# A fused mLSTM cell and tanh-shrink MLP on one core: the steady part begins at the first half-done group instead of the second

## The chip, the cores and the metric

The kernel runs on one core of one Trainium2 chip. The metric is device time in microseconds (us) of one execution, the median of several; lower is better. PE is the engine that multiplies matrices, PEld its weight loads, DVE the vector engine, ACT the scalar engine with the activation functions, POOL the general engine, SP the engine whose queue here only issues transfers. Each engine works through its own list of instructions in the order in which they stand. Matrix products land in banks of PSUM, and ACT or DVE must have read a bank before PE may fill it again.

## The reference

Two stages follow each other. The first is an mLSTM cell over 4 batches, 8 heads, 768 time steps and head size 40; the second is an MLP over the 3072 rows of 320 numbers that the cell gives.

```python
for t in range(S):                                   # per batch and head
    m_new  = max(f[t] + m, i[t])
    f_stab = exp(f[t] + m - m_new);  i_stab = exp(i[t] - m_new);  m = m_new
    C = f_stab * C + i_stab * outer(v[t], k[t])
    n = f_stab * n + i_stab * k[t]
    y[t] = sigmoid(o_gate[t]) * (C @ q[t]) / max(|n . q[t]|, 1)
x = y.transpose(0, 2, 1, 3).reshape(B * S, H * D)    # 3072 x 320
h = x @ w_in                                         # 320 x 2048
out = (h - tanh(h)) @ w_out                          # 2048 x 320
```

The weights come as 64-bit floats; the kernel turns them into 32-bit floats on the chip.

## The kernel before

**Units, groups, pairs, items.** The cell is cut into 24 units, each 128 time steps of one batch with all heads; unit n is time block n // 4 of batch n % 4. Two units make a group of 256 rows of x, so there are 12 groups, 0 to 11. The 2048 columns of `w_in` are cut into 8 pairs of 128-column blocks, 0 to 7. One group times one pair is a run, and PE works on items of two runs (the first two items have one): the products with `w_in` (called up, into the PSUM banks `ph_up`, one for each block of a pair), then h - tanh(h) as a polynomial on ACT and DVE, then the products with `w_out` (called down, into `po` or `pS`). There are 49 items. On the rows of x of a small group, `RUNS` walks along diagonals: items 0 to 8 hold pairs 0 to 3 of groups 0 to 3, items 9 and 10 pairs 4 to 7 of group 0, items 11 and 12 those of group 1, 13 and 14 of group 2, 15 and 16 of group 3; from item 17 on each group has four items.

**The polynomial.** For an item ACT computes z (`square`) and q (`again`) from `ph_up`; DVE computes `gt<-ph_up,z` twice (here called the cubes; the first cube is the last reader of the first `ph_up` bank, so the next item's first product waits for it), then `gt<-q,gt` twice. Pairs 4 to 7, and all pairs from group 4 on, use a scheme of seven products in place of eight for down: DVE first forms four sums of gt (`s1` to `s4`, in `sums_of_g`) and, once for each pair of `w_out`, four differences of blocks of it (`wT`, in `sums_of_weights`). `put_together` makes the output `ob` of a group from the banks `pS` and, for groups 0 to 3, from the parts of pairs 0 to 3 (`part`).

**Planned part and steady part.** The first part of the program is laid out by a planner (`Plan`): it holds operations with estimated times, ranks, tokens for buffers, and it records them in the order in which its own model starts them. It covers the weights' conversion from 64 bits, the units below `PLANNED`, and the items below `START`. Where it finds PE idle, it puts in products that compute nothing (`awake`). From item `START` on a loop walks item by item in a fixed order, and DVE's and ACT's other work (the list `work`) is merged in at places that are given in items. `START` is the item that holds run (`TAIL`, `SPLIT`), so `TAIL`, 2 and `SPLIT` 4 make it item 13.

**What differs in the steady part.** There x is split into two parts, x and l, with their difference d (`split_x`), the weights of a pair into high, low and cross parts (`split_in`: four steps, ACT, DVE, ACT, DVE), and up is 24 products in a faster number format (names `x_thirds`, `thirds`, `w_thirds`, `w_high`) plus eight halves in place of eight full products plus halves (`in_thirds`). The products of x and of l come first, those of d last; between them ACT rescales each bank (`ph_up<-ph_up`). An item falls back to full products if its pairs are not split by then. Pairs 4 and 5 are split in the planned part, 6 half there, 7 and 0 to 3 in the steady part. A pair's low and cross part are eight blocks of 128 x 128 that need homes in memory that something else has left (`homes`).

A unit, too, is computed in another way in the steady part: `crossed_scores` (tile `ps`) in one item and `block_turned` (tiles `pT`, `pc`) in the next, with `turn_back` and `gate_turned` on DVE and two trips through memory (`h_rows`, `z_in` and `y_rows`, `xT`) in place of the products that the planned part spends on turning. `cell_slot` sets, in 21 places over two items, where the parts of the unit before (its gates) come.

**Order on the queues.** Within each engine the order is pinned as recorded. SP issues the loads of the planned units and the units' trips through memory; POOL issues the loads of weights, of the units in the steady part, and the stores of `ob`.

Of the kernel before, what the change touches and what calls it, by code (L numbers as in the profile page):

```python
# [49 lines left out]
FP = mybir.dt.float32  # L50
# [11 lines left out]
L = 128  # L62
# [26 lines left out]
def kernel(  # L89
# [215 lines left out]
    FIRST, SPLIT, PLANNED, TAIL = 4, 4, 10, 2  # L305
# [65 lines left out]
    padded = {}  # L371

    def load_unit(n, names=("kz", "qz", "v", "k", "o", "q2"), queue=SP, behind=(), crossed=False):
# [3 lines left out]
        for name in names:  # L377
# [3 lines left out]
            elif name in ("kz", "qz"):  # L381
                t[name] = load.tile([128, HH, L], FP, name=name, tag=f"{name}{n % 3 if n < PLANNED and not general else n % 2}", bufs=1)
# [298 lines left out]
    def scaled(n, i, name, bufs, by_heads=False):  # L681

        t = un[n]
        flat = padded["vs"][n % 4] if t["crossed"] else att.tile([L, H * D1 + HALF - D1], FP, name=name, tag="P" if general else name, bufs=bufs)
# [217 lines left out]
    def turn_back(n):  # L902
# [3 lines left out]
        both = att.tile([128, 2, HH * L // BLOCK, BLOCK], FP, name="zt", tag="P", bufs=4)  # L906
# [12 lines left out]
        t["z"] = att.tile([L, 2, H, BLOCK], FP, name="z_in", tag="P", bufs=4)  # L919
# [31 lines left out]
    def cell_slot(s, o):  # L951
# [12 lines left out]
        steps += 6 * pause  # L964
# [4 lines left out]
        return steps + 4 * pause  # L969
# [168 lines left out]
    def homes(p):  # L1138

        def at(tag, pool=const, n=4):  # L1140
            if tag not in places:
                places[tag] = pool.tile([128, n, 128], FR, name="w_thirds", tag=tag, **({} if pool is const else {"bufs": 1}))

        if p == 4:
            at("space", n=9)
        elif p == 5:
            at("kz2", load)
            at("qz2", load)
        elif p == 6:
            at("part0", n=5)  # L1150
            at("q2", n=9)
        elif p == 7:
            at("diag")
            for b in range(2):
                at(f"state{(PLANNED + b) % B}", n=2)
        elif p == 0:
            for b in range(2, B):
                at(f"state{(PLANNED + b) % B}", n=2)
            at("part1", n=5)
        elif p == 1:  # L1160
            at("xT2", n=6)
        elif p == 2:
            at("xT3", n=6)
            at("part2", n=5)
        else:
            at("part3", n=5)
        four = range(4)
        blocks = [(tag, n) for tag, ns in (
            (*((f"state{(PLANNED + b) % B}", range(2)) for b in (2, 3)), ("part1", four)),
            (("xT2", range(6)), ("part0", (4,)), ("part1", (4,))),  # L1170
            (("xT3", four), ("part2", four)),
            (("part3", four), ("xT3", (4, 5)), ("part2", (4,)), ("part3", (4,))),
            (("space", range(8)),),
            (("kz2", four), ("qz2", four)),
            (("part0", four), ("q2", (6, 7, 8)), ("space", (8,))),
            (("diag", four), *((f"state{(PLANNED + b) % B}", range(2)) for b in (0, 1))))[p] for n in ns]
        return blocks[0:4], blocks[4:8]
# [523 lines left out]
    def plan_thirds():  # L1701
# [328 lines left out]
```

## Time and profile before

| | us |
|---|---|
| median of 3 runs | 499.57 (498.94 to 509.22) |
| profiled execution, its own time | 495.56 |
| span of the profiled execution, first to last instruction | 493.8 |
| around the span | 1.8 |
| first product of item 13, the first of the steady part | 165.4 from the span's start |
| first product of item 20 | 231.4 |
| first product of item 48, the last | 474.7 |

A span begins at 0. A row of the timeline has the start, the time, the engine, the program's names of what is written and read, and how many instructions were merged; in brackets the idle time before it and what ended that. Products overlap, so what a stretch of PE takes is read from the start of its first row to the start of the row behind it, not from the sum of the times; the same holds for DVE, whose instructions overlap by some 0.08 us. A number behind an x in a timeline counts instructions as the chip ran them, where a full 32-bit product is two; the lists of order count it once.

Where PE's units stand in the span: its busy share by 40 equal slices is 9 tenths or more in each but the last, and DVE's is lower.

```
PE   9999999999999999999999999999999999999995
DVE  5999969998977697999897886996995988775734
ACT  4566597676455435455454544444545445454541
POOL 4523304320003341523423423431241100000000
```

### The profile page before, as it was taken

To read this page: it belongs to the slowest core of one execution; us is meant where nothing else is said; L and a number is where in the kernel's file an instruction comes from. 1 tells how busy PE (TensorE), PEld (TensorE's weight loads), DVE (VectorE), ACT (ScalarE), POOL (GpSimd) and SP (SyncE) were. 2 spreads that over 40 slices of the span, in tenths; PEclk is the share of its full clock that TensorE was granted. 3 is DMA by queue.
4 is the path that set the end of the run, shared out by engine and by line. 5 is a ranking of instruction groups with operands and counts; after the bars stand their busy time and mean duration, and the time that the engine had idled before them with its cause. 6 is when DMAs were issued, how large, how long until landed. Compare 5 with 4: busy or idle time off the path is not lost.

```text
span 493.8 us, 12474 instructions
## 1 busy us (share of the span) xinstructions
PE 483.7 (98%) x4715; PEld 431.1 (87%) x4715; DVE 400.8 (81%) x913; ACT 256.2 (52%) x609; POOL 119.3 (24%) x221
## 2 busy tenths in 40 slices
PE   9999999999999999999999999999999999999995
PEld 5778888787788898898999999999999999999995
DVE  5999969998977697999897886996995988775734
ACT  4566597676435455545454444544545445454541
POOL 4523304320003341523423423431241100000000
PEclk9999999999999999999999999999999999999998
DMA  7987625740001223355346436444444432420001
GB/s 232 286 261 246 191 71 142 149 136 7 7 1 35 61 65 74 101 118 125 81 98 140 99 83 137 99 98 103 95 112 83 94 82 44 75 60 1 27 1 33
DMA packets 116902, 48.82 MB, mean 99 GB/s; under 512 B 96872, under 2 KB 109064, under 8 KB 116836
## 3 DMA queue, kind: packets, MB, share of 16 engines
q1 hardware_dynamic: 107132, 23.21, 23.1%
q0 software_dynamic: 9504, 24.43, 16.4%
q8 instruction: 39, 0.64, 0.5%
q10 hardware_dynamic: 200, 0.33, 0.2%
q14 instruction: 27, 0.22, 0.1%
HBM read 37.30 MB, written 10.35 MB: 97 GB/s over the span
## 4 chain that ended last, share of the span: by engine, by line
PE 88%; DVE 6%; ACT 2%; DMA 1%; issue 1%; SPq 0%; DVEq 0%; ACTq 0%
PE ph_up L138 36%; PE pS L138 29%; PE po L138 7%; PE ph L138 4%; PE ps L138 3%; PE awake L138 3%; PE pT L138 3%; PE pc L138 2%; DVE gt L115 1%; DVE s L115 1%; PE px L142 1%; DVE w_thirds L115 1%; DMA h_rows<-zt 1%; DVE zt L115 1%; ACT q L115 0%
## 5 line engine op out<-in xcount | busy, mean ns | idle before, releaser
L115 ACT ACTIVATE z<-ph_up 128x512 f32<-128x512 f32 (+1 forms) x98 | 56.8, 583 | 102.5 <-PE ph_up L138 97.0
L115 ACT ACTIVATE ph_up<-ph_up 128x512 f32<-128x512 f32 x70 | 40.7, 582 | 82.4 <-PE ph_up L138 79.1
L115 DVE SCALAR_TENSOR_TENSOR gt<-ph_up,z 128x512 f32<-128x512 f32 (+1 forms) x98 | 62.7, 671 | 22.9 <-ACT z L115 22.7
L138 PE MATMUL pS<-wT,s 128*128 128x160 f32 x480 | 71.9, 299 | 0.0
L138 PEld LDWEIGHTS pS<-wT,s 128*128 128x128 f32 x480 | 67.4, 190 | 0.3 <-issue 0.2
L115 ACT ACTIVATE q<-z,tiny 128x512 f32<-128x512 f32 (+1 forms) x98 | 65.8, 711 | 0.7
L115 DVE SCALAR_TENSOR_TENSOR gt<-q,gt 128x512 f32<-128x512 f32 (+1 forms) x98 | 63.5, 677 | 0.0
L115 POOL DMA_DIRECT2D out<-ob x11 | 8.0, 727 | 220.6 <-DVE ob L115 220.6
L138 PE MATMUL pS<-w_out,gt 128*128 128x160 f32 x320 | 58.4, 312 | 0.0
L138 PE MATMUL ph_up<-xT,w_half 64*64 64x256 f32 (+1 forms) x608 | 53.6, 393 | 0.0
L138 PEld LDWEIGHTS pS<-w_out,gt 128*128 128x128 f32 x320 | 45.4, 189 | 5.4 <-issue 3.6
L138 PE MATMUL ph_up<-x_thirds,w_high 128*128 128x256 f32 x280 | 47.9, 293 | 2.0 <-DVE gt L115 2.0
L138 PE MATMUL ph_up<-xT,w_in 128*128 128x256 f32 x208 | 49.0, 382 | 0.0
L138 PE MATMUL ph_up<-x_thirds,w_thirds 128*128 128x256 f32 x280 | 44.4, 281 | 0.0
L138 PEld LDWEIGHTS ph_up<-xT,w_in 128*128 128x128 f32 x208 | 38.5, 190 | 5.4
L138 PEld LDWEIGHTS ph_up<-x_thirds,w_high 128*128 128x128 f32 x280 | 38.5, 188 | 2.7 <-PE pS L138 2.1
L138 PE MATMUL ph_up<-thirds,w_thirds 128*128 128x256 f32 x250 | 39.8, 292 | 0.2 <-ACT ph_up L115 0.2
L138 PEld LDWEIGHTS ph_up<-xT,w_half 64*64 64x64 f32 (+1 forms) x608 | 28.1, 146 | 12.9 <-issue 3.7
L138 PE MATMUL po<-w_out,gt 128*128 128x320 f32 x128 | 38.2, 441 | 0.0
L138 PEld LDWEIGHTS ph_up<-x_thirds,w_thirds 128*128 128x128 f32 x280 | 37.9, 188 | 0.0
L138 PEld LDWEIGHTS ph_up<-thirds,w_thirds 128*128 128x128 f32 x250 | 33.3, 189 | 0.4 <-ACT ph_up L115 0.4
L138 PEld LDWEIGHTS po<-w_out,gt 128*128 128x128 f32 x128 | 23.1, 190 | 8.7 <-issue 0.7
(143 smaller groups left out, 870.0 us busy)
## 6 DMA issues: line engine op xcount, KB each, us to landing
w<-in_moe_w_out POOLq DMA_DIRECT2D x8, 640.0 KB, 6.4
w<-in_moe_w_in POOLq DMA_DIRECT2D x16, 256.0 KB, 4.7
h_rows<-zt SPq DMA_DIRECT2D x56, 64.0 KB
z_in<-h_rows SPq DMA_DIRECT2D x56, 64.0 KB
out<-ob POOLq DMA_DIRECT2D x11, 320.0 KB, 2.7
y_rows<-yt SPq DMA_DIRECT2D x56, 48.0 KB
xT<-y_rows SPq DMA_DIRECT2D x28, 96.0 KB
kz<-in_kT POOLq DMA_DIRECT2D x26, 80.0 KB, 2.8
```

Source lines behind the costliest of these rows:

```text
L115: i = method(*args, **kwargs)
L138: return cls.keep(nc.tensor.matmul(*args, **kwargs))
L142: return cls.keep(nc.tensor.transpose(*args, **kwargs))
```

## The change

The steady part now begins at item 11 (`TAIL` 1) and takes over unit 9 (`PLANNED` 9). The rest follows from this or goes with it:

- x's parts get another home: x in `P3`, one of four buffers of the units, which are now named one by one and taken in turn (`next_p`), four in the planned part and three in the steady part; l in `xT0`. `xT1` holds group 1, which is still in use.
- The parts of pairs 5, 6, 7 and 0 to 3 get other homes, and are begun at other places, in items from `START`: pairs 0 to 3 at 1.6, 2.6, 4.4 and 5.4 (2.0, 3.0, 5.4 and 6.6 before). Most pairs' parts lie in fewer pieces, so one instruction takes the place of two or three. `s1` and `s3` share a buffer, since pair 5 takes the one of `s3`.
- The differences of `w_out` for pairs 0 to 3 (16 instructions on DVE) leave the planned part, and stand in the steady part at 2.2, 3.7, 5.5 and 6.3 items from `START`.
- In `cell_slot` the gates come two places of 21 later, with two pauses fewer behind them.

```diff
-    FIRST, SPLIT, PLANNED, TAIL = 4, 4, 10, 2
+    FIRST, SPLIT, PLANNED, TAIL = 4, 4, 9, 1
...
-    padded = {}
+    padded, turns_of_p = {}, [0, 4]
+
+    def next_p():
+        turns_of_p[0] += 1
+        return f"P{turns_of_p[0] % turns_of_p[1]}"
...
-        un[n]["P"] = att.tile([L, 2, HH, L], FP, name="P", tag="P", bufs=4)
+        un[n]["P"] = att.tile([L, 2, HH, L], FP, name="P", tag=next_p(), bufs=1)
...
-        steps += 6 * pause
+        steps += 8 * pause
...
-        return steps + 4 * pause
+        return steps + 2 * pause
...
-        s1, s2, s3 = (conv.tile([128, 2, L], FP, name=name, tag=tag, bufs=2)[:, 0:len(some)]
-                      for name, tag in (("s1", "w_e"), ("s2", "w_m"), ("s3", "w_r")))
+        two = conv.tile([128, 2, 2, L], FP, name="s1", tag="w_e", bufs=2)
+        s1, s3 = two[:, 0, 0:len(some)], two[:, 1, 0:len(some)]
+        s2 = conv.tile([128, 2, L], FP, name="s2", tag="w_m", bufs=2)[:, 0:len(some)]
...
         elif p == 5:
-            at("kz2", load)
-            at("qz2", load)
+            for name in ("one", "two"):
+                at(name, 5, conv, "w_r", 2)
...
-        x, l = (const.tile([128, NK + 1, TG], FR, name="x_thirds", tag=f"xT{k}") for k in range(2))
+        x = att.tile([128, NK + 1, TG], FR, name="x_thirds", tag="P3", bufs=1)
+        l = const.tile([128, NK + 1, TG], FR, name="x_thirds", tag="xT0")
...
-                              ([op] if op else [converted[p, 0], *seconds, *([results[0]] if p == 6 else [])]) + ([uses] if i == 2 else []), 60.0 if i < 2 else -12.0)
+                              ([op] if op else [*converted.values(), *seconds]) + ([uses] if i == 2 else []), 60.0 if i < 2 else -12.0)
...
-        op = None
-        for p in range(SPLIT):
-            steps_of_p = []
-            for i in range(2):
-                op = plan.add("V", 0.65, lambda p=p, i=i, steps=steps_of_p: [steps.extend([] if i else sums_of_weights(p)), *[step() for _, step in steps[2 * i:2 * i + 2]]],
-                              [op] if op else [made[NP - 1]], 70.0)
...
+    turns_of_p[1] = 3
...
-    for p, x0 in ((6, -0.25), (7, 0.1), (0, 2.0), (1, 3.0), (2, 5.4), (3, 6.6)):
+    for p, x0 in ((6, -0.25), (7, 0.1), (0, 1.6), (1, 2.6), (2, 4.4), (3, 5.4)):
...
+    for p, x0 in ((0, 2.2), (1, 3.7), (2, 5.5), (3, 6.3)):
+        sums_of_p = []
+        for i in range(4):
+            work[START + int(x0 + 0.15 * i)].append((START + x0 + 0.15 * i, 0.0, lambda p=p, i=i, steps=sums_of_p: [steps.extend(() if i else sums_of_weights(p)), steps[i][1]()]))
```

What this moves is shown at three places. The first is PE's list at the end of the planned part. Before, item 12's up is followed by the beginning of item 11's down (`pS_1681`, `pS_1683`), and then by twenty `awake` products, each with its own weight load; this is where they begin:

```order
L138 MATMUL pS_1552<-w_out,s_1601 128x160 x2
L138 MATMUL ph_up<-xT,w_in 128x256 x8
L138 MATMUL ph_up<-xT,w_half 128x256 x4
L138 MATMUL pS_1681<-w_out,gt 128x160 x4
L138 MATMUL pS_1683<-wT,gt 128x160 x2
L138 LDWEIGHTS diag
L138 MATMUL awake<-diag 128x512
```

The same engine now, behind item 8's down: the second of two `awake`, item 10's up, item 9's down (`pS_1478` to `pS_1480`), and with the third row from the end the steady part begins, at item 11:

```order
L138 LDWEIGHTS diag
L138 MATMUL awake<-diag 128x512
L138 MATMUL ph_up<-xT,w_in 128x256 x8
L138 MATMUL ph_up<-xT,w_half 128x256 x4
L138 MATMUL pS_1478<-w_out,gt 128x160 x4
L138 MATMUL pS_1480<-wT,gt 128x160 x2
L138 MATMUL pS_1479<-wT,s_1463 128x160 x4
L138 MATMUL pS_1478<-wT,s_1464 128x160 x2
L138 MATMUL pS_1480<-w_out,s_1465 128x160 x2
L138 MATMUL ph_up<-x_thirds,w_high 128x256 x4
L138 MATMUL ph_up<-x_thirds,w_thirds 128x256 x4
L138 MATMUL ph_up<-x_thirds,w_high 128x256 x4
```

So no filler stands between the last planned down and the steady part. Over the whole list `awake` goes from 63 to 42 products; items 11, 12 and 18 change from full products to split ones; and unit 9's products change from the planned to the steady kind.

The second place is ACT's list where the steady part begins. Before, the upper part of x of the first steady group (`x_thirds<-xT`) stands behind item 10's polynomial, two items ahead of its use:

```order
L115 ACTIVATE z,sums<-ph_up 128x512
L115 ACTIVATE q<-z,tiny 128x512
L115 ACTIVATE z,sums<-ph_up 128x512
L115 ACTIVATE q<-z,tiny 128x512
L115 ACTIVATE x_thirds<-xT 128x768
L115 COPY w_high<-w_thirds 128x512 x2
```

Now it stands behind item 10's polynomial again, but item 10 is the last planned item, and the copies to `w_high` of pairs 4 and 5 stand ahead of it:

```order
L115 COPY w_high<-w_thirds 128x512
L115 ACTIVATE z,sums<-ph_up 128x512
L115 COPY w_high<-w_thirds 128x512
L115 ACTIVATE q<-z,tiny 128x512
L115 ACTIVATE z,sums<-ph_up 128x512
L115 ACTIVATE q<-z,tiny 128x512
L115 ACTIVATE x_thirds<-xT 128x768
L115 COPY vs<-crossed 128x8
```

So the first steady item needs what ACT does last in the planned part.

The third place is DVE's list from the sums of item 16 to the cubes of item 17. Before:

```order
L115 TENSOR_TENSOR s_2375<-s_2374,gt 128x256
L115 TENSOR_TENSOR s_2377<-gt,s_2375 128x256
L115 TENSOR_TENSOR P<-ps,over 128x384 x2
L115 TENSOR_TENSOR vs<-v,crossed 128x8x40
L115 SCALAR_TENSOR_TENSOR gt<-ph_up,z 128x512 x2
```

Now the differences of `w_out` of pairs 2 and 3 and the last step of pair 3's parts stand in between:

```order
L115 TENSOR_TENSOR s_2437<-gt,s_2436 128x256
L115 TENSOR_TENSOR wT<-w_out,wT 128x160
L115 SCALAR_TENSOR_TENSOR w_thirds<-w_thirds 128x512
L115 TENSOR_TENSOR wT<-w_out 128x160
L115 TENSOR_TENSOR wT<-w_out,wT 128x160
L115 TENSOR_TENSOR P<-ps,over 128x384 x2
L115 TENSOR_TENSOR vs<-v,crossed 128x8x40
L115 TENSOR_TENSOR wT<-w_out 128x160
L115 SCALAR_TENSOR_TENSOR gt<-ph_up,z 128x512
L115 TENSOR_TENSOR wT<-w_out,wT 128x160
L115 SCALAR_TENSOR_TENSOR gt<-ph_up,z 128x512
```

So the first cube comes five instructions later behind the sums, and another one stands between the two cubes.

More of the change, by code (lines that the diff above doesn't have):

```diff
@@ L381, in load_unit @@
             elif name in ("kz", "qz"):
-                t[name] = load.tile([128, HH, L], FP, name=name, tag=f"{name}{n % 3 if n < PLANNED and not general else n % 2}", bufs=1)
+                t[name] = load.tile([128, HH, L], FP, name=name, tag=f"{name}{(n + 1) % 3 if n < PLANNED and not general else n % 2}", bufs=1)
                 for i in range(2):
@@ L905, in turn_back @@
         t = un[n]
-        both = att.tile([128, 2, HH * L // BLOCK, BLOCK], FP, name="zt", tag="P", bufs=4)
+        both = att.tile([128, 2, HH * L // BLOCK, BLOCK], FP, name="zt", tag=next_p(), bufs=1)
         zt, added = both[:, 0], both[:, 1].rearrange("p b i -> p (b i)")
@@ L1138, in homes, with at @@
     def homes(p):
-        def at(tag, pool=const, n=4):
-            if tag not in places:
-                places[tag] = pool.tile([128, n, 128], FR, name="w_thirds", tag=tag, **({} if pool is const else {"bufs": 1}))
+        def at(name, n=4, pool=const, tag=None, bufs=1):
+            if name not in places:
+                places[name] = pool.tile([128, n, 128], FR, name="w_thirds", tag=tag or name, **({} if pool is const else {"bufs": bufs}))
+        first, second, third, fourth = (f"state{(PLANNED + i) % B}" for i in range(B))
@@ L1144, in homes @@
         if p == 4:
-            at("space", n=9)
+            at("space", 9)
         elif p == 5:
-            at("kz2", load)
-            at("qz2", load)
+            for name in ("one", "two"):
+                at(name, 5, conv, "w_r", 2)
         elif p == 6:
-            at("part0", n=5)
-            at("q2", n=9)
+            at("kz2", 4, load)
+            at("qz2", 4, load)
         elif p == 7:
             at("diag")
-            for b in range(2):
-                at(f"state{(PLANNED + b) % B}", n=2)
+            at(first, 2)
@@ L1156, in homes @@
+            at(second, 2)
         elif p == 0:
-            for b in range(2, B):
-                at(f"state{(PLANNED + b) % B}", n=2)
-            at("part1", n=5)
+            at("part0", 5)
         elif p == 1:
-            at("xT2", n=6)
+            at(third, 2)
+            at(fourth, 2)
+            at("xT1", 6)
         elif p == 2:
-            at("xT3", n=6)
-            at("part2", n=5)
-        else:
[L1166 to L1172, printed above, removed]
+            at("xT2", 6)
+        else:
+            at("part1", 5)
+            at("part2", 5)
@@ L1173, in homes @@
+        two, four = range(2), range(4)
+        blocks = [(name, n) for name, ns in (
+            (("part0", four), ("q2", (6, 7, 8)), ("part0", (4,))),
+            ((third, two), (fourth, two), ("xT1", four)),
+            (("xT2", range(6)), ("xT1", (4, 5))),
+            (("part1", four), ("part2", four)),
             (("space", range(8)),),
+            (("one", four), ("two", four)),
             (("kz2", four), ("qz2", four)),
-            (("part0", four), ("q2", (6, 7, 8)), ("space", (8,))),
@@ L1176, in homes @@
-            (("diag", four), *((f"state{(PLANNED + b) % B}", range(2)) for b in (0, 1))))[p] for n in ns]
+            (("diag", four), (first, two), (second, two)))[p] for n in ns]
         return blocks[0:4], blocks[4:8]
@@ L1893, in keep_any @@
         decay = eT[:, n].unsqueeze(2).to_broadcast([TOP, H, D1])
-        own = att.tile([TOP, H, D1], FP, name="own", tag="P", bufs=4)
+        own = att.tile([TOP, H, D1], FP, name="own", tag=next_p(), bufs=1)
         V.memset(own, 1.0)
```

10 lines of the change are left out of this document (5 added, 5 removed).

## The prediction

> **What bounds the kernel now.** I read the page's busy times first, then PE's waits, the sums by stage, and then the timelines of PE and DVE around the start of the steady part.
>
> ```profile
> PE 483.7 (98%) x4715; PEld 431.1 (87%) x4715; DVE 400.8 (81%) x913; ACT 256.2 (52%) x609; POOL 119.3 (24%) x221
> PE ph_up L138 <- DVE gt L115: 2.0, 3, 0.9
> 95.50:165.40 69.90, 69.90 (x398) 55.68 (x395) 60.77 (x133) 38.33 (x90) 12.12 (x31) 1.00 0.17 48
> 165.40:231.40 66.00, 63.57 (x782) 58.60 (x782) 57.47 (x134) 34.89 (x87) 21.67 (x39) 1.00 0.38 91
> 231.40:303.80 72.40, 72.38 (x929) 68.57 (x929) 60.49 (x145) 35.21 (x83) 26.00 (x46) 1.00 0.48 106
> ```
>
> PE bounds the kernel: 483.7 of 493.8 us. The next line is the largest of its waits, three times for DVE's gt. The last three are stages: length, then busy time (and count) of PE, PEld, DVE, ACT and POOL, the granted clock, the DMA share and GB/s. The end of the planned part (95.5 to 165.4) has PE without a gap, but some of that is `awake`, which computes nothing. Items 13 to 19 (165.4 to 231.4) have all the waits, with DVE busy for 57.5 of 66.0 us; from item 20 on PE is never without work. So a gain has to come from PE's own time or from those waits, and DVE is the engine that can give it back.
>
> **The planned part.**
>
> ```profile
> 95.56 1.06 PE L138 MATMUL ps<-qz,kz 40*128 40x128 f32 x16
> ...
> 121.03 0.55 PE L142 MATMUL px<-ident,ys 128*128 128x128 f32 x3
> ...
> 134.75 1.03 PE L138 MATMUL awake<-diag 128*128 128x512 bf16 x4
> 135.61 3.62 PE L138 MATMUL ph_up<-xT,w_in 128*128 128x256 f32 x16
> ...
> 141.96 1.79 PE L138 MATMUL pS<-wT,s 128*128 128x160 f32 x12
> ...
> 144.13 3.62 PE L138 MATMUL ph_up<-xT,w_in 128*128 128x256 f32 x16
> ...
> 158.99 4.48 PE L138 MATMUL awake<-diag 128*128 128x512 bf16 x20
> 163.31 1.79 PE L138 MATMUL pS<-wT,s 128*128 128x160 f32 x12
> 164.94 0.71 PE L138 MATMUL pS<-w_out,s 128*128 128x160 f32 x4
> 165.38 0.74 PE L138 MATMUL ph_up<-x_thirds,w_high 128*128 128x256 f32 x4
> ```
>
> Up to 95.56 PE's list is the same. Unit 9's planned products go: nine rows between 95.56 (`ps`, 0.98 to the next start) and 121.03 (`px`, 0.39), together 4.36 from start to start. Items 11 and 12 with items 10's and 11's down go (144.13 to 158.99 and 163.31 to 165.38): 14.86 + 2.07 = 16.93. Of 24 `awake` in this stretch three stay; 20 take 4.32 (158.99 to 163.31), so 0.216 each, and 21 give 4.53. The sum is 25.8, and item 11 could begin at 165.38 - 25.82 = 139.56, if PE alone decides.
>
> Unit 9's rows and one `awake`, 4.36 + 0.22, stand ahead of item 9's sums, so PE would want these at 141.96 - 4.6 = 137.4.
>
> ```profile
> 136.44 0.42 DVE L115 TENSOR_TENSOR s<-gt,s 128x256 f32<-128x256 f32 x1
> ```
>
> DVE had the last of them at 136.86, five us to spare. Ahead of them it loses unit 9's state, gates and scaling, two differences of `w_out` and one part of a pair's weights, 3.5 us by their rows, so it has them at 133.4 if its own list decides, with four to spare. The end that costs nothing is 0. The other end is that the conversions of the weights come no sooner than before, since they wait for transfers: then the sums end at 136.9 again, three steps on parts of pairs, item 10's polynomial and l follow, 5.6 together, and l comes at 142.5 in place of 140.1, some 2.4 us lost. I take 0: PE waits for DVE nowhere between 95.5 and 158.99.
>
> At item 11 there is a wait. PE's last planned up ends at 135.65; behind it ACT does z, a copy, q, z, q and then the upper part of x.
>
> ```profile
> 148.84 0.60 ACT L115 ACTIVATE z<-ph_up 128x512 f32<-128x512 f32 x1 [0.44 <-PE ph_up L138]
> ...
> 150.19 0.58 ACT L115 ACTIVATE z<-ph_up 128x512 f32<-128x512 f32 x1
> ```
>
> The first z and q with what stands between take 150.19 - 148.84 = 1.35 from start to start. With 0.6 for the copy and 0.8 for x (by DVE's 768 columns of it, below) the upper part ends at 135.75 + 2 x 1.35 + 0.6 + 0.8 = 139.85, and l follows on DVE at 140.9. PE wants x at 139.56 and l at 140.1, so it waits about 0.7 in all. Before, x was ready two items ahead. The ends of this wait are 0 and the 2.4 above.
>
> **The items that come back, and item 18.**
>
> ```profile
> 174.37 0.73 PE L138 MATMUL ph_up<-x_thirds,w_high 128*128 128x256 f32 x4
> ...
> 177.18 0.51 PE L138 MATMUL ph_up<-thirds 128*128 128x256 f32 x2 [0.20 <-ACT ph_up L115]
> ...
> 178.77 0.62 PE L138 MATMUL pT<-qz,state 40*64 40x128 f32 x16
> ...
> 191.92 0.71 PE L138 MATMUL pS<-w_out,s 128*128 128x160 f32 x4
> 193.38 0.71 PE L138 MATMUL ph_up<-x_thirds,w_high 128*128 128x256 f32 x4 [0.76 <-DVE gt L115]
> ...
> 201.91 0.71 PE L138 MATMUL pS<-w_out,s 128*128 128x160 f32 x4
> 202.98 0.74 PE L138 MATMUL ph_up<-x_thirds,w_high 128*128 128x256 f32 x4 [0.36 <-DVE gt L115]
> ...
> 212.71 3.62 PE L138 MATMUL ph_up<-xT,w_in 128*128 128x256 f32 x16
> ...
> 217.17 0.62 PE L138 MATMUL pT<-qz,state 40*64 40x128 f32 x16
> ...
> 229.79 0.71 PE L138 MATMUL pS<-w_out,s 128*128 128x160 f32 x4
> 231.42 0.71 PE L138 MATMUL ph_up<-x_thirds,w_high 128*128 128x256 f32 x4 [0.93 <-DVE gt L115]
> ```
>
> An undisturbed steady item with half a unit in it takes 174.37 - 165.38 = 8.99; items 11 and 12 with unit 9 so cost 17.98, against 21.29 in the planned kind. Item 13 then begins at 139.56 + 0.7 + 17.98 = 158.24, that is 7.1 sooner. Item 18 changes from full to split products: its up takes 217.17 - 212.71 = 4.46 now, item 14's 178.77 - 174.37 = 4.40 with a wait of 0.20 in it, so 0.3 is gained. The other work of items 13 to 48 is the same on PE.
>
> The waits of before: `pS<-w_out,s` takes 0.44 to the next start where nothing waits (164.94 to 165.38), and 1.46, 1.07 and 1.63 ahead of items 16, 17 and 20. That is 1.02 + 0.63 + 1.19 = 2.84 that could go.
>
> **DVE in the steady part.** This is where I expect part of it back.
>
> ```profile
> 127.94 0.32 DVE L115 TENSOR_TENSOR wT<-w_out 128x160 f32<-128x160 f32 x1
> 128.30 0.33 DVE L115 TENSOR_TENSOR wT<-w_out,wT 128x160 f32<-128x160 f32 x1
> 128.54 0.32 DVE L115 TENSOR_TENSOR wT<-w_out 128x160 f32<-128x160 f32 x1
> ...
> 189.23 1.02 DVE L115 TENSOR_TENSOR P<-ps,over 128x384 f32<-128x384 f32 x2 [1.04 <-PE ps L138]
> ...
> 191.87 0.76 DVE L115 SCALAR_TENSOR_TENSOR w_thirds<-w_thirds 128x256 fp32r<-128x256 f32 x2 [1.23 <-ACT w_high L115]
> 192.55 1.28 DVE L115 SCALAR_TENSOR_TENSOR gt<-ph_up,z 128x512 f32<-128x512 f32 x2
> 193.75 1.28 DVE L115 SCALAR_TENSOR_TENSOR gt<-q,gt 128x512 f32<-128x512 f32 x2
> 194.95 0.75 DVE L115 TENSOR_TENSOR s<-gt 128x256 f32<-128x256 f32 x2
> ...
> 215.67 0.48 DVE L115 TENSOR_TENSOR ob<-pS,a 128x320 f32<-128x320 f32 x1
> ...
> 217.47 0.83 DVE L115 TENSOR_TENSOR ob<-ob,part 128x640 f32<-128x640 f32 x1
> L115 DVE TENSOR_TENSOR thirds<-x_thirds 128x768 fp32r<-128x768 f32 x2 | 1.9, 948 | 0.0
> ```
>
> From start to start a cube is 0.60, a `gt<-q,gt` 0.60, a difference 0.24 to 0.36, a step of half a pair's parts 0.34 to 0.40. An item's polynomial and sums come to 4.0 to 4.4, the output of one of groups 0 to 3 to 2.4, the split of a group's x to 1.7, a pair's parts to 1.4, and a unit to 5 over two items. With these I summed DVE's order from each item's cubes to the next one's: after the change 8.0, 11.1, 9.0, 10.8, 9.0, 12.1 and 7.8 us for items 11 to 17, together 67.7, and then 8.2, 5.9, 9.0, 6.7. PE needs 9.0 an item, so 63 for these seven. (Before, items 13 to 19 have 8.0, 9.3, 9.5, 9.3, 8.0, 9.6, 7.1, so 60.8.) Three groups' outputs and x in pairs of items, six pairs' parts and the 16 differences now fall together.
>
> An excess costs PE only when the first cube comes after PE has done the item's down. At item 12 that leaves 1.5 us, and item 11 adds 1.0. Item 12's excess (11.1 - 9.0) uses this up; item 13 is level, but its step on pair 1's parts waits some 1.2 for ACT, whose first step on them stands behind item 13's q, and so item 14 waits 0.9. Item 14's excess then goes straight to item 16: 1.75. Item 16's (3.1) makes item 17's d of x 0.6 late and item 18's first product 2.45. From then on DVE needs less than PE. The sum is 5.7. The ends: 0, as from item 20 on before; and 12.5, if DVE's waits of before (1.23 for ACT, 1.04 for `ps`, above) come back at each of four pairs' parts and three units, 8.0 in place of the 1.2 that I have, with no slack to take them. I take 5.7: it is nearest to the rows of items 15 to 19, where PE waited 2.84 although DVE had less to do than PE.
>
> The gates two places later: DVE meets `z_in` later and POOL and SP issue the same transfers; x of a group is wanted some 5 us after it lands, of which the shift takes 1.7. Nothing, and at most the 0.4 that DVE once waited for `z_in` between items 17 and 18. The buffers (three in place of four, the homes) add waits only on work that is an item old: nothing.
>
> **A rule against it.** The granted clock is 1.00 in the three stages above, with PE's waits of up to 1.2 us and 24 `awake` products in the first. The Trainium skill (TensorE: Matmul & The Clock Gate, section "Why this matters for your kernels") asks for no idle gaps of PE beyond about 3 us between bursts, since an idle window takes the clock to half. By that rule the waits at items 17 and 18 would halve the clock for a window if they ran together to 3 us; by the window of 3.4 us that the page gives (section "What's actually happening") the sum would then be about 3.4 us worse, an estimate from that page. As I have them, 0.6 and 2.45 with an item's products between, the rule takes nothing. No trace here shows a gap that long.
>
> **The sum.** -7.1 (start of item 13) - 0.3 (item 18) - 2.84 (old waits) + 5.7 (new ones) = -4.6 us on a span of 493.8: 489.2. The profiled execution took 495.56 and would take 491.0. The median of the runs, 499.57, lies 4.0 above it, with runs from 498.94 to 509.22; I carry the difference over and predict 495.0.
>
> **Rivals.**
>
> - DVE's excess is hidden: the cube's slack is larger than I have it, or the order of DVE's list happens to fit. For it speaks that item 18 before had 9.6 on DVE against 9.0 of PE and item 19 began without a wait; against it that PE waited three times with less on DVE. Then -7.1 - 0.3 - 2.84 = -10.2, and 489.3.
> - Slower than before: DVE's queue loses time to waits in order, and what it loses goes to PE, as there is no slack. With the upper end of 12.5 in place of 5.7 it is -4.6 + 6.8 = +2.2, and 501.8. For it speaks that ACT's copies of the parts now stand ahead of its rescaling of a bank, so that one late step delays both; against it that many of DVE's waits of before fell where it was early anyway. It decides from 4.6 us of further waits on.
> - The start is set by DVE and the weights, not by PE: l comes 2.4 us later, as in the bound above, and the rest as forecast: 497.4.
> - The clock falls to half once in items 16 to 18, behind the longest wait, and an up of 4.4 (174.37 to 178.77) takes twice its time: 499.4. The row for it is the granted clock, which is 1.00 through all waits so far.
> - The change gives what it takes: more steady items but as many waits more, between 498 and 501.
>
> **How the numbers follow.** The forecast has 0.50 (its own range 492.5 to 497.5), the hidden excess 0.14, the slower one 0.13, the late start 0.14, the clock 0.04, nothing gained 0.05. The range 489.5 to 501 leaves out half of the hidden excess and most of the slower case, somewhat under 0.2 in all. A measurement of this kernel can tell about 2% from no change, which is 10 us: faster by that means below 489.6, half of the hidden excess and a little for the spread of the runs, 0.10; slower means above 509.6, 0.03; within, 0.87.
>
> **What would show it.** Right: item 11's first split product at 139 to 141 us, item 13's at about 158, no fillers between item 9's down and item 11; PE waiting for DVE's gt ahead of items 14, 16 and 18, most ahead of 18, and none from item 20 on; item 20 at 226 to 227. Wrong: item 11 after 142 (DVE or weights late), PE's waits between items 12 and 19 below 2 or above 9 us, a clock below 1.00 there, or waits on `xT` or `z_in` from item 20 on.

## The result, and the profile after

| | before | changed |
|---|---|---|
| median of 6 runs, us | 499.22 | 493.26 |
| ratio, 95% interval | | 0.9896 (0.9865 to 0.9928) |
| the same again, 6 runs beside 11 | 499.60 | 492.55; 0.987 (0.9835 to 0.9905) |
| profiled execution, its span | 495.56, 493.8 | 492.65, 490.9 |
| item 13 begins | 165.38 | 158.48 |
| item 20 begins | 231.42 | 227.32 |

The kernel is 1.0 to 1.3% faster, a change that is smaller than 2%, and the interval of each measurement lies below 1. The forecast was 495.0 us, a ratio of 0.991. In some executions some 9 us more pass early in the span (in three traces below, within the first 32 us); the ratios leave such executions out, the medians do not.

The page's busy times of the changed kernel, in the prediction's order:

```profile
PE 476.0 (97%) x4783; PEld 426.6 (87%) x4783; DVE 405.9 (83%) x918; ACT 256.8 (52%) x600; POOL 125.1 (25%) x230
```

Its waits of PE (total, times, longest):

```profile
PE ph_up L138 <- DVE gt L115: 4.1, 3, 1.8
...
PE ph_up L138 <- DVE x_thirds L115: 0.6, 1, 0.6
...
PE ph_up L138 <- DVE thirds L115: 0.4, 1, 0.4
...
PE pS L138 <- DVE s L115: 0.2, 1, 0.2
```

Its stages, cut where item 11 and item 20 begin (columns as in the prediction: length, then busy time and count of PE, PEld, DVE, ACT, POOL, the granted clock, DMA share, GB/s):

```profile
95.50:139.70 44.20, 44.20 (x224) 34.25 (x222) 39.37 (x81) 26.50 (x59) 9.85 (x28) 1.00 0.21 64
139.70:227.30 87.60, 82.02 (x1021) 75.90 (x1021) 82.84 (x194) 46.34 (x112) 28.52 (x51) 1.00 0.37 88
227.30:299.70 72.40, 72.40 (x932) 68.59 (x930) 59.70 (x141) 34.58 (x80) 26.00 (x46) 1.00 0.51 110
```

PE's work fell by 7.7 us, and its waits for gt doubled. The second row shows where: in items 11 to 19 DVE is busy for 82.84 of 87.60 us, more than PE.

PE's timeline of the changed kernel, at the start of the steady part and at its waits:

```profile
137.42 1.79 PE L138 MATMUL pS<-wT,s 128*128 128x160 f32 x12
139.05 0.71 PE L138 MATMUL pS<-w_out,s 128*128 128x160 f32 x4
139.72 0.74 PE L138 MATMUL ph_up<-x_thirds,w_high 128*128 128x256 f32 x4
141.03 0.74 PE L138 MATMUL ph_up<-x_thirds,w_thirds 128*128 128x256 f32 x4 [0.57 <-DVE x_thirds L115]
...
158.48 0.74 PE L138 MATMUL ph_up<-x_thirds,w_high 128*128 128x256 f32 x4
...
168.62 0.71 PE L138 MATMUL ph_up<-x_thirds,w_high 128*128 128x256 f32 x4 [0.81 <-DVE gt L115]
...
188.54 0.71 PE L138 MATMUL ph_up<-x_thirds,w_high 128*128 128x256 f32 x4 [1.48 <-DVE gt L115]
...
201.25 0.36 PE L138 MATMUL ph_up<-thirds 128*128 128x256 f32 x1 [0.37 <-DVE thirds L115]
...
209.82 0.70 PE L138 MATMUL ph_up<-x_thirds,w_high 128*128 128x256 f32 x4 [1.78 <-DVE gt L115]
...
227.32 0.74 PE L138 MATMUL ph_up<-x_thirds,w_high 128*128 128x256 f32 x4
```

Item 11 begins at 139.72 behind item 9's sums, item 13 at 158.48, and PE waits ahead of items 14, 16 and 18 and in item 17. Where did the 6.9 us of item 13 go? 2.8 of them are lost between items 13 and 20.

The waits of DVE in the changed kernel between items 11 and 20 (total, times, longest), and where its cubes of items 13 to 18 begin:

```profile
DVE P L115 <- PE ps L138: 1.5, 2, 1.2
DVE w_thirds L115 <- ACT w_thirds L115: 0.8, 1, 0.8
```

```profile
167.79 1.28 DVE L115 SCALAR_TENSOR_TENSOR gt<-ph_up,z 128x512 f32<-128x512 f32 x2
...
176.98 1.28 DVE L115 SCALAR_TENSOR_TENSOR gt<-ph_up,z 128x512 f32<-128x512 f32 x2
...
187.70 1.28 DVE L115 SCALAR_TENSOR_TENSOR gt<-ph_up,z 128x512 f32<-128x512 f32 x2
...
196.90 1.28 DVE L115 SCALAR_TENSOR_TENSOR gt<-ph_up,z 128x512 f32<-128x512 f32 x2
...
208.99 0.68 DVE L115 SCALAR_TENSOR_TENSOR gt<-ph_up,z 128x512 f32<-128x512 f32 x1
...
216.87 1.28 DVE L115 SCALAR_TENSOR_TENSOR gt<-ph_up,z 128x512 f32<-128x512 f32 x2
```

All these waits end before 167.79 but one of 0.36 at 224.74. So from the cubes of item 13 to those of item 18 DVE goes from one instruction to the next without waiting. From one item's cubes to the next one's it takes 9.19, 10.72, 9.20, 12.09 and 7.88 us; the prediction's sums of its work for items 13 to 17 were 9.0, 10.8, 9.0, 12.1 and 7.8.

The chain of waits that ended last (start, length, what was waited for; its longest steps) runs over DVE from 180 us up to item 18's first product:

```profile
207.42 1.02 DVE P L115 x2
209.07 0.61 DVE gt L115
209.82 2.12 PE ph_up L138 x16
```

From 209.82 on it is PE's.

### The profile page after: what moved, and what is told of

Same layout as the page of the kernel before. It is cut to its first block, busy times and chain, and to the rows that moved or that the text cites. A ratio compares the mean times of both kernels' runs of the same rounds, so it can differ in the third digit from the quotient of the medians.

```text
span 490.9 us, 12662 instructions
## 1 busy us (share of the span) xinstructions
PE 476.0 (97%) x4783; PEld 426.6 (87%) x4783; DVE 405.9 (83%) x918; ACT 256.8 (52%) x600; POOL 125.1 (25%) x230
## 4 chain that ended last, share of the span: by engine, by line
PE 80%; DVE 11%; DMA 4%; issue 2%; ACT 1%; POOL 1%; SPq 0%; DVEq 0%
PE ph_up L138 34%; PE pS L138 26%; PE po L138 7%; PE ph L138 3%; DVE gt L115 3%; PE ps L138 3%; PE pT L138 3%; DMA w<-in_moe_w_in 2%; PE pc L138 2%; DVE s L115 2%; DVE w_thirds L115 1%; DVE zt L115 1%; DVE x_thirds L115 1%; DVE ob L115 1%; DMA h_rows<-zt 1%
## 5 line engine op out<-in xcount | busy, mean ns | idle before, releaser
L115 ACT ACTIVATE ph_up<-ph_up 128x512 f32<-128x512 f32 x76 | 44.2, 582 | 87.0 <-PE ph_up L138 83.4
L138 PE MATMUL ph_up<-x_thirds,w_high 128*128 128x256 f32 x304 | 52.0, 293 | 4.1 <-DVE gt L115 4.1
L138 PE MATMUL ph_up<-x_thirds,w_thirds 128*128 128x256 f32 x304 | 48.4, 281 | 0.6 <-DVE x_thirds L115 0.6
L138 PEld LDWEIGHTS ph_up<-x_thirds,w_high 128*128 128x128 f32 x304 | 41.6, 188 | 5.1 <-issue 3.7
L138 PE MATMUL ph_up<-thirds,w_thirds 128*128 128x256 f32 x280 | 44.1, 292 | 0.4 <-ACT ph_up L115 0.4
L138 PEld LDWEIGHTS ph_up<-x_thirds,w_thirds 128*128 128x128 f32 x304 | 41.2, 188 | 0.8 <-DVE x_thirds L115 0.8
L138 PE MATMUL ph_up<-xT,w_in 128*128 128x256 f32 x160 | 38.3, 383 | 0.0
L138 PEld LDWEIGHTS ph_up<-thirds,w_thirds 128*128 128x128 f32 x280 | 37.1, 189 | 0.8 <-ACT ph_up L115 0.8
L138 PEld LDWEIGHTS ph_up<-xT,w_in 128*128 128x128 f32 x160 | 29.5, 190 | 4.3
```

The costliest lines, as they stand in the source:

```text
L115: i = method(*args, **kwargs)
L138: return cls.keep(nc.tensor.matmul(*args, **kwargs))
```

## The experiments

An item's length is taken from its first up product to that of the next. In the two kernels that were traced twice, items 11 to 19 take the same time within 0.1 us (87.60 twice for the changed one, 84.16 and 84.06 for the best), while the beginning and the end of the span do not; so the time from the start of item 11 to that of item 20, in one trace of each kernel, is compared, beside the medians. Each ratio is to the kernel before on the same chip; the medians come from several chips and can't all be compared with each other.

| kernel | item 11 begins | item 20 begins | between | median | ratio to before |
|---|---|---|---|---|---|
| changed | 139.72 | 227.32 | 87.60 | 493.26 | 0.9896 (0.9865 to 0.9928) |
| differences on POOL | 141.81 | 230.00 | 88.19 | 495.12 | 0.992 (0.9875 to 0.9966) |
| differences later | 149.08 | 236.53 | 87.45 | 493.34 | 0.9875 (0.9789 to 0.996) |
| differences twice | 140.31 | 233.67 | 93.36 | 498.80 | 0.9998 (0.9958 to 1.0039) |
| gates at their old places | 139.49 | 226.78 | 87.29 | 499.46 (1 run) | |
| differences planned | 139.30 | 225.78 | 86.48 | 491.18 | 0.9799 (0.9715 to 0.9882) |
| x sooner | 148.99 | 235.81 | 86.82 | 501.54 (4 runs, 491.05 to 503.32) | |
| ACT's step sooner | 139.62 | 226.44 | 86.82 | 491.08 (1 run) | |
| three edits | 141.57 | 227.16 | 85.59 | 491.40 | 0.9805 (0.9712 to 0.9898) |
| hybrid | 139.48 | 223.64 | 84.16 | 490.27 | 0.9801 (0.9702 to 0.9899) |

The theory was that the new waits come from the amount of DVE's work in items 12 to 17 ("load"); the rival, that they come from single instructions of DVE that stand in its list and wait for another engine ("order").

**The differences on POOL.**

```diff
-    def sums_of_weights(p):
+    def sums_of_weights(p, engine=V):
...
-        return [(1.0, lambda o=o, a=a, b=b: V.tensor_tensor(out=o, in0=a, in1=b, op=sub)) for o, a, b in (
+        return [(1.0, lambda o=o, a=a, b=b: engine.tensor_tensor(out=o, in0=a, in1=b, op=sub)) for o, a, b in (
...
-            work[START + int(x0 + 0.15 * i)].append((START + x0 + 0.15 * i, 0.0, lambda p=p, i=i, steps=sums_of_p: [steps.extend(() if i else sums_of_weights(p)), steps[i][1]()]))
+            work[START + int(x0 + 0.15 * i)].append((START + x0 + 0.15 * i, 0.0, lambda p=p, i=i, steps=sums_of_p: [steps.extend(() if i else sums_of_weights(p, G)), steps[i][1]()]))
```

> The changed kernel with the 16 differences of w_out for pairs 0 to 3 on POOL in place of DVE, at the same places. Load theory (the waits ahead of items 14, 16 and 18 are DVE's excess over PE in items 12 to 17): DVE loses 16 x 0.3 = 4.8 us of work there, so most of the 4.9 us (1.07 + 1.75 + 2.05) of these waits goes; PE's waits for gt between items 12 and 19 fall from 4.1 to below 1, item 20 begins at 223 to 224 in place of 227.3, and the run is 3.5 to 4.5 us shorter than the changed kernel. Order theory (the waits are set by single DVE instructions that wait in order for ACT, POOL or PE, and the differences only fill the time): the waits fall by less than 1, item 20 at 226.5 or later. Third: POOL is slower at them or slows DVE beside it; then PE waits for wT or for P of POOL, and the gain is below 2.

Nothing is gained: 88.19 in place of 87.60. These items in a row by stage:

```profile
141.81:230.00 88.19, 82.70 (x1021) 76.00 (x1021) 83.19 (x178) 46.49 (x112) 38.71 (x67) 1.00 0.37 86
```

DVE has 16 instructions of 0.32 us fewer (178 in place of 194), and is busy as long as in the changed kernel. Its sums in the changed kernel (shortest, median and longest in ns, first and last start):

```profile
L115 DVE TENSOR_TENSOR s<-gt x18: 417/419/421, 141.9 to 222.6; 128x256 f32<-128x256 f32 x18
L115 DVE TENSOR_TENSOR s<-s,gt x9: 424/426/426, 142.7 to 223.0; 128x256 f32<-128x256 f32 x9
```

The same with the differences on POOL, and a piece of the timeline of that run:

```profile
L115 DVE TENSOR_TENSOR s<-gt x18: 410/416/1146, 144.0 to 225.0; 128x256 f32<-128x256 f32 x18
L115 DVE TENSOR_TENSOR s<-s,gt x9: 424/425/747, 144.8 to 225.4; 128x256 f32<-128x256 f32 x9
```

```profile
185.54 1.81 DVE L115 TENSOR_TENSOR s<-gt 128x256 f32<-128x256 f32 x2
...
186.52 0.54 POOL L115 TENSOR_TENSOR wT<-w_out 128x160 f32<-128x160 f32 x1
187.01 0.72 POOL L115 TENSOR_TENSOR wT<-w_out,wT 128x160 f32<-128x160 f32 x1
187.39 0.62 DVE L115 TENSOR_TENSOR s<-s,gt 128x256 f32<-128x256 f32 x1
```

Two sums that take 0.75 together take 1.81 where POOL's differences run beside them. The third case of the expectation holds: POOL slows DVE by about what it takes off it. PE then waits for DVE's sums (0.86 and 0.24 us) and not for wT, as that case had it. With no load taken off, this run can't decide between load and order.

**The differences later.** `((0, 2.2), (1, 3.7), (2, 5.5), (3, 6.3))` becomes `((0, 4.8), (1, 6.45), (2, 7.0), (3, 7.6))`.

> The changed kernel with the same 16 differences still on DVE but later, at 4.8, 6.45, 7.0 and 7.6 items from START in place of 2.2, 3.7, 5.5 and 6.3, nearer to the downs that need them (items 17 and 18). Load theory: the work of item 12, 14 and 16 falls to 9.9, 9.6 and 9.7 us, that of items 17 and 18, which have the least, rises; the waits ahead of 14, 16 and 18 fall from 4.9 to 1 to 2 in all, something of 0.5 to 1 appears ahead of items 19 or 20, item 20 begins at 224 to 225. Order theory: less than 1 us of change, item 20 at 226.5 or later. If the new places are too late, PE waits for wT in the down of item 17 or 18.

A miss: 87.45. Item 15 falls from 10.82 to 9.99 and item 17 from 12.18 to 10.99, but item 16 rises from 9.10 to 10.09 and item 19 from 8.54 to 9.39. That the sum hardly changes is what the order theory said; but DVE doesn't wait between the cubes of item 13 and those of item 18, and moved inside a stretch that is full, work costs the same elsewhere. And item 13 stays at 10.15 though pair 0's differences have left it, so the wait ahead of item 14 is not their doing.

**The differences twice.** `steps[i][1]()` in that loop becomes `[steps[i][1]() for _ in range(2)]`.

> The changed kernel with each of the 16 differences of w_out of pairs 0 to 3 made twice in a row on DVE, 4 to 4.8 us more of DVE's work in items 12 to 17 and nothing else. Load theory: no slack is left, so PE loses nearly all of it: waits for gt rise from 4.1 to about 8, item 20 begins at 231 to 232 and the run is 3.7 to 4.8 us longer. Order theory: part of the added work fits into time in which DVE waits; less than 2 us longer, item 20 before 229.3.

Items 11 to 19 take 5.76 us more; the load theory holds for what is added. 4.5 of it are waits, what sixteen more differences take at 0.28 each (0.24 to 0.36 from start to start). The rest is PE's clock. Two waits of PE in this run:

```profile
191.09 0.71 PE L138 MATMUL ph_up<-x_thirds,w_high 128*128 128x256 f32 x4 [2.56 <-DVE gt L115]
...
214.86 1.19 PE L138 MATMUL ph_up<-x_thirds,w_high 128*128 128x256 f32 x4 [3.21 <-DVE gt L115]
```

And four microseconds behind each:

```profile
191.00:195.00 4.00, 3.91 (x36) 3.75 (x40) 3.86 (x10) 2.00 (x4) 0.00 (x0) 1.00 0.40 66
```

```profile
214.00:218.00 4.00, 3.14 (x16) 3.17 (x16) 3.93 (x10) 0.58 (x1) 0.00 (x0) 0.57 0.39 62
```

Behind an idle time of 2.56 us the granted clock is 1.00 and four products take 0.71; behind 3.21 it is 0.57 and they take 1.19. Item 18 takes 10.27 in place of 8.97, so this costs 1.3.

**The upper part of x sooner.** In `plan_thirds` the operation no longer waits for the ups of group 0:

```diff
-                     [units[n]["x"] for n in (TAIL * GT, TAIL * GT + 1)] + [ups[x] for x in range(START) if any(run[0] < 1 for run in items[x])] + seconds, 50.0)
+                     [units[n]["x"] for n in (TAIL * GT, TAIL * GT + 1)] + seconds, 50.0)
```

> The changed kernel with the upper part of x of the first steady group planned without waiting for item 10's up, so ACT makes it some us sooner, ahead of item 10's polynomial. Both theories: the wait of 0.57 us for l in item 11 goes and item 12 begins at 148.9 to 149.0 in place of 149.54. Load theory: DVE is full from item 12 on, so most of this is lost again ahead of item 14 or 16; item 20 begins at most 0.3 sooner, and the time is the same within 0.4 us. Order theory: item 20 is 0.6 sooner.

Item 11 takes 8.99 in place of 9.82. Items 12 to 17 are as in the changed kernel within 0.02 and item 18 takes 0.05 more, so 0.78 of the 0.83 is kept. My load theory was wrong here: DVE is not yet full in item 11. Its `P<-ps` waits there for PE's `ps` (1.18 us in the changed kernel, 0.82 in this run), and so it begins 0.82 sooner too, counted from item 11's start.

**The gates at their old places.** 6 pauses ahead and 4 behind in `cell_slot`.

> The changed kernel with the gates back at their old places (6 pauses ahead, 4 behind). The prediction put nothing on this part of the change. So: item lengths from 11 to 20 the same within 0.3 us in sum (87.60 in the changed kernel), at most a DVE wait for z_in of up to 0.4. Rival: the gates' place matters because DVE is full here; then the waits ahead of items 14, 16 and 18 change by more than 0.5 each.

The sum over items 11 to 19 is 0.31 less, and PE's idle times ahead of items 16 and 17 move by 0.5 and 0.2, so up to item 20 the new places gain nothing. But this execution took 499.46 us, and the loss lies behind item 20. DVE's waits between items 20 and 48 (total, times, longest), in the kernel before:

```profile
DVE den L115 <- DMA z_in<-h_rows: 17.7, 12, 2.9
```

In the changed kernel:

```profile
DVE den L115 <- DMA z_in<-h_rows: 6.9, 8, 1.6
```

In the changed kernel with the gates back:

```profile
DVE den L115 <- DMA z_in<-h_rows: 33.5, 11, 8.0
```

These waits for a unit's trip through memory cost PE nothing while each is short: the kernel before had 17.7 us of them with no wait of PE. With one of 8.0 PE stood still for 3.75 us ahead of item 25, and items 24 and 25 took 5.6 longer. How much the new places spare DVE is not shown, since the wait differs much between traces: 6.9 to 16.8 us in eleven with the new places; with the old ones 17.7 in the kernel before, 25.7 in that kernel without its fillers and 33.5 here. Whether such a late transfer is common with the old places a single execution can't tell.

**The differences planned.** The sixteen go back into `plan_thirds` with rank 70, as in the kernel before. Two now stand between item 10's cubes, and 14 behind its sums.

> The changed kernel with the 16 differences of w_out for pairs 0 to 3 back in the planner's hands as in the kernel before, where 14 of them now stand behind item 10's sums, in a stretch in which DVE of the changed kernel is idle for 2.7 us of item 10 and 1.3 of item 11. Nothing runs on POOL. Load theory, as refined by the run with POOL (POOL's work beside DVE made DVE's instructions longer by about what was taken off): with the 4.8 us off DVE in items 12 to 17 and nothing beside it, the waits ahead of 16 and 18 fall by 2.5 to 3.5 in all, that ahead of 14 stays (it is DVE's wait for ACT's step on pair 1); items 11 to 19 together take 84 to 85.5 in place of 87.60, with up to 1 us of new waiting in item 11 or 12. Order theory: they take more than 86.8.

86.48, so 1.12 gained and not the 2 to 3.6 expected. Items 15 and 17 take 9.99 and 10.52 in place of 10.82 and 12.18 (PE's idle time ahead of items 16 and 18 falls by 0.82 and 1.07), but item 11 takes 11.03 in place of 9.82, since not all of the differences fit into DVE's idle time there. Item 13 stays at 10.16: the differences of pair 0 stood ahead of DVE's wait for ACT, so nothing is gained by taking them out.

**The fillers of the kernel before.** The line that issues the products `awake` beside begun items is left out of the kernel before; nothing that it computes changes. It takes out the 24 between 134 and 164 us and seven more at 26.2 us.

> The kernel before without the 24 filler products (awake) between 134 and 164 us, which compute nothing. The prediction counted 21 of them as 4.5 us of PE's time that the change saves. If they were pure cost, item 13 begins 4.5 to 5.2 us sooner behind item 12's up, without PE waiting there. If they covered a wait (as the planner has it: PE would have nothing to do until DVE has item 11's and 12's sums), PE now waits in their place, item 13 begins as before within 0.5 us, and the time is that of the kernel before; then the change did not save the fillers but filled the same wait with the steady part's products. By the Trainium skill (TensorE: Matmul & The Clock Gate, section on what is actually happening) a PE idle for longer than its window of about 3.4 us would get half the clock afterwards, so the granted clock behind a wait of 4.3 us may fall.

Ratio to before 1.0022 (0.997 to 1.0074): no difference. PE where the twenty fillers stood:

```profile
157.45 1.35 PE L138 MATMUL pS<-w_out,gt 128*128 128x160 f32 x8
158.64 0.71 PE L138 MATMUL pS<-wT,gt 128*128 128x160 f32 x4
162.28 3.48 PE L138 MATMUL pS<-wT,s 128*128 128x160 f32 x12 [2.93 <-DVE s L115]
165.59 0.71 PE L138 MATMUL pS<-w_out,s 128*128 128x160 f32 x4
166.03 0.74 PE L138 MATMUL ph_up<-x_thirds,w_high 128*128 128x256 f32 x4
```

And the clock behind the wait:

```profile
162.00:166.00 4.00, 3.72 (x15) 3.73 (x16) 2.50 (x7) 0.00 (x0) 3.21 (x7) 0.57 0.47 104
```

Of the 4.32 us of fillers 3.1 covered a wait for DVE's sums of item 11 (162.28 - 158.64, less the 0.54 from start to start that the row at 158.64 takes undisturbed). Without them twelve products take 3.48 in place of 1.79, at a granted clock of 0.57, and item 12 takes 13.19 in place of 12.73. So the fillers alone were not 4.3 us to be had: most of them stood in a wait. The changed kernel has products of the steady part there.

**ACT's step sooner.** For pair 1 the first `dx` is -0.4 in place of 0.0, so that ACT's first step on its parts stands ahead of item 13's polynomial.

> The changed kernel with one step moved: ACT's first step on pair 1's parts 0.4 items sooner, so that it stands ahead of item 13's polynomial and not behind it. Order theory for item 14: DVE's wait of 0.76 for this step, which stands ahead of item 13's cubes, is what makes PE wait 0.81 (1.07 from start to start); it goes, and item 13 takes 9.2 to 9.4 in place of 10.14. What is gained there is lost in part ahead of item 16 if DVE's load decides there: items 11 to 19 together take 86.8 to 87.3 in place of 87.60. Load theory for item 14 too: no change of item 13's 10.14.

Item 13 takes 9.40 in place of 10.14, the profile shows no idle time of PE ahead of item 14, and all of it stays: 86.82. So the order theory holds for item 14. The wait that it removes, in DVE's timeline of the changed kernel:

```profile
167.08 0.80 DVE L115 TENSOR_TENSOR w_thirds<-w_in,w_thirds 128x256 fp32r<-128x256 f32 x2 [0.76 <-ACT w_thirds L115]
```

**Three edits together** (x sooner, ACT's step sooner, differences planned).

> Three edits of the runs above together, on the changed kernel: the upper part of x sooner, ACT's first step on pair 1 sooner, and the 16 differences of w_out for pairs 0 to 3 in the planner's hands. Alone they took items 11 to 19 from 87.60 us to 86.82, 86.82 and 86.48. If the chain from item 11 to 19 runs through DVE, so that a microsecond taken out of it anywhere is a microsecond gained, they add up: 87.60 - 0.78 - 0.78 - 1.12 = 84.9. If each only uncovers the next wait, less: above 86. The planned differences should also cost less at item 12 than the 1.2 us that they cost alone, since l is made earlier and DVE's idle time in item 10 grows: then 84.0 to 84.9.

85.59: they do not quite add up, since item 11 still takes 11.09. The planned differences cost 2.1 there once l no longer hides part of them.

**The hybrid.** The same three edits, but only the differences of pairs 0 and 1 are planned, and those of pairs 2 and 3 come in item 18:

```diff
-    for p, x0 in ((0, 2.2), (1, 3.7), (2, 5.5), (3, 6.3)):
+    for p, x0 in ((2, 7.0), (3, 7.6)):
...
+        for p in range(2):
+            steps_of_p = []
+            for i in range(2):
+                op = plan.add("V", 0.65, lambda p=p, i=i, steps=steps_of_p: [steps.extend([] if i else sums_of_weights(p)), *[step() for _, step in steps[2 * i:2 * i + 2]]],
+                              [op] if op else [made[NP - 1]], 70.0)
```

> As the run with three edits, but only the differences for pairs 0 and 1 in the planner's hands, in the time that DVE has left in item 10; those for pairs 2 and 3 stay in the steady part and come later, at 7.0 and 7.6 items from START, in item 18, behind which DVE has time (5.9 to 8.2 us of work in items 18 and 19). If DVE's work between the cubes decides, item 11 loses nothing (9.0), items 15 to 17 are as with planned differences (10.0, 9.2, 10.5) and item 19 gets 0.6 to 0.9 longer: 83.5 to 84.5 for items 11 to 19. If the steady part's late differences cost as much as in the run with later places (item 18 waited 1.18, item 19 took 9.39), 85 to 86, no better than the three edits.

84.16, as expected for the sum, with item 11 at 8.99; items 16 and 19 take 9.41 and 8.94, where 9.2 and 9.1 to 9.4 were expected. PE's waits for gt in the hybrid:

```profile
PE ph_up L138 <- DVE gt L115: 1.5, 3, 0.7
```

**The changed kernel and the hybrid again,** side by side with the kernel before.

> The changed kernel once more, beside the kernel before and the hybrid on the same chip. By its runs so far 0.9896 of the kernel before (0.9865 to 0.9928); by the starts of its items 11 and 20, which change little between executions, items 11 to 19 take 87.6 us.

> The hybrid once more, with more runs. Its items 10 to 19 took 92.57 us against 96.25 of the changed kernel, so it should be 3.7 us shorter than that: 0.982 of the kernel before if the changed one is at 0.9896, and an interval that lies below that of the changed kernel.

The changed kernel is at 0.987 (0.9835 to 0.9905), with 87.60 again; the hybrid at 0.982 (0.9774 to 0.9867), with 84.06. The traces show 3.5 us less between items 11 and 20 and 0.24 in item 10; the ratios differ by 0.5%, 2.5 us in place of the 3.7 expected, and their intervals overlap by 0.3%, where they were expected apart. So the hybrid is faster than the kernel before; that it is faster than the changed one the traces show and the times do not yet.

## Why the prediction was right

- **Item 13's start.** Forecast 7.1 sooner, measured 6.9. The sum of PE's rows gave 139.56 for item 11 and it began at 139.72; DVE had item 9's sums in time, since the row at 137.42 has no wait. The wait for x and l was put at 0.7; item 11 takes 9.82 against an undisturbed 8.99, so it is 0.83. But the 4.53 for the fillers can't be had by leaving them out: the run without them shows that PE then waits 3.1. It came true here because in the changed kernel DVE has item 9's sums at 132.46, five us ahead of the row that reads them at 137.42. The prediction had checked just these sums (133.4), and so stood on the right condition, but it called the fillers work that goes.
- **New waits.** Forecast 0.9 ahead of item 14, 1.75 ahead of 16, 0.6 in item 17, 2.45 ahead of 18, in sum 5.7. From start to start, less what each row takes undisturbed (0.44 ahead of an item), they are 1.07, 1.75, 0.97 (0.63 and 0.34, at the two idle times of item 17) and 2.05: 5.8. The run with ACT's step sooner shows that the cause given for item 14, a DVE step that waits for ACT, was right. Ahead of 16 and 18 the load decides: DVE has no wait there, its work came out within 0.2 us of the prediction's sum for each item, the differences made twice cost in full, and planned they take 0.82 and 1.07 off these two waits.
- **Old waits and item 18.** -2.84 and -0.3. From item 13 to 20 the changed kernel takes 68.84 (227.32 - 158.48) against 66.04: 2.80 more. Less their waits the seven items take 63.20 before (66.04 - 2.84) and 63.00 now (68.84 - 5.84): the old waits went, and 0.2 of the 0.3 is there. Item 18 by itself hardly shows it (8.99 and 8.97), as a row of item 17's down (`pS<-wT,gt`, 0.44 at 211.77) stands inside its up now and stood ahead of it before.
- **The end.** At item 20 the change stood at -4.1 (forecast -4.6), and the last result on DVE at 484.20 + 0.49 against 488.32 + 0.49, still -4.1. The span fell by 2.9 only, since from there to its end 6.2 us passed in this execution and 5.0 in that of the kernel before. In the second trace of the changed kernel it is 5.5, and the span 490.1, so this differs between executions of one kernel. The prediction had no term for it; what sets it was not tried.
- **The median.** The span was forecast at 489.2 and is 490.9, the median at 495.0 and is 493.26. The term that was off is the 4.0 us between profiled execution and median that was carried over from the kernel before: here it is 0.6. The span came out 1.7 above its forecast and the median 1.7 below, so that the median is this near is in part luck; the forecast of PE's starts is not.
- **The gates.** Forecast nothing, with an upper end of 0.4. Up to item 20 that is so. Behind it DVE's waits for `z_in` are 10.8 us less than before, which PE had not felt. The upper end looks too small: with a late transfer 5.6 us were lost in one execution with the old places, and the longest of these waits with the new ones is 2.9.
- **Rivals.** The hidden excess is out: 5.8 us of waits. Of the slower case, DVE's waits in order, one of 0.76 decided something. The start was not set by DVE and the weights (0.57); that rival's 497.4 also counted its 2.4 us on top of the 0.7 that the forecast already has, and should have been 496.7. The clock was 1.00 in all three stages, with idle times of up to 1.78 us; in the runs where it fell, that cost 1.3 to 1.7 us and not the 4.4 of that rival. That as much is lost as gained is out too: the times are below 498.

From the cubes of item 13 to item 18 the steady part runs at DVE's pace. Work moved inside that stretch gained nothing, and work added cost its full time. Of the two waits that were removed nearly all was gained (0.78 us each). Of the 4.5 us of differences moved to where DVE idles 1.1 came back, and in the hybrid 1.9 (3.44 less the two 0.78), since some stood ahead of a wait for ACT and some cost item 11 or item 19.

## What to carry to other kernels

When a change starts the fast part of a kernel sooner, add up the other engine's work in that part over several steps and not one; where it exceeds the bound engine's and no slack is left, what is moved in comes back as a wait. Before counting filler products as a gain, ask what the engine would have waited for without them. And a wait of a busy engine for another's small step, found in its timeline, was here a cheaper gain than moving its load.

## What the hardware showed

POOL's and DVE's work side by side does not add up to more work done. The timeline of DVE and POOL in the run with the differences on POOL, ahead of item 18:

```profile
209.36 1.02 DVE L115 SCALAR_TENSOR_TENSOR w_thirds<-w_thirds 128x512 fp32r<-128x512 f32 x1
209.79 0.97 POOL L115 TENSOR_TENSOR wT<-w_out 128x160 f32<-128x160 f32 x1
210.30 1.01 DVE L115 TENSOR_TENSOR P<-ps,over 128x384 f32<-128x384 f32 x2
210.72 0.52 POOL L115 TENSOR_TENSOR wT<-w_out,wT 128x160 f32<-128x160 f32 x1
```

DVE's step on the weights, with both inputs in the core's own memory (SBUF), takes 1.02 in place of the 0.68 that it takes in the changed kernel, and POOL's difference beside it 0.97; `P<-ps,over`, which reads a bank of PSUM, keeps its 1.01 for two, and POOL's beside it takes 0.52. The Trainium skill (SBUF — State Buffer, section "SBUF: two separate sides") says that POOL and a DVE instruction with two such inputs take a shared pair of ports in turn, each for a whole instruction; the trace agrees.

The clock fell to 0.57 over four microseconds behind PE's idle times of 2.93 and 3.21 us, and not behind 2.56; in the run with the gates back it was 0.83 over ten behind 3.75. The Trainium skill (TensorE: Matmul & The Clock Gate, section "What's actually happening") gives a free-running window of about 3.4 us; here somewhat less was enough. The loss was 1.7, 1.3 and, for item 25 in the run with the gates back, 1.6 us (10.68 in place of 9.07), not the 3.4 of the estimate in the prediction: by the same window, half the clock over 3.4 us leaves an estimated 1.7 us of products undone, so the prediction's was twice too large.
